# Coarser squares and sums, and buffer fills moved from DVE to POOL, in a fused cosine attention and channel MLP kernel

## The chip, the cores and the metric

The kernel runs on one core of one Trainium2 chip. The metric is the device time of one execution in microseconds (us). A profile covers one execution; its span (602.4 us for the kernel before) is some 1.8 us shorter than the time of the same run. Engines are called as the profile calls them: PE does matrix products, DVE vector work, ACT activation functions and copies, POOL general work and some of the DMA issues, SP DMA issues only.

## The reference

For each of 8 batches and 12 heads, with 448 tokens of 64 elements, the rows of q and k are divided by their norms, scores over tau = 0.1 go through a softmax, and v is averaged by it. The result, as 448 x 768 per batch, goes through a rank-32 mixing of tokens and an MLP over channels (768 to 3072 and back).

```python
q_n = q / (norm(q) + 1e-06); k_n = k / (norm(k) + 1e-06)
attn = softmax(q_n @ k_n.T / tau)
x = heads_side_by_side(attn @ v)              # (8, 448, 768)
u = x + ((x.T @ U) @ V).T
out = u + relu(u @ w_ch1) @ w_ch2             # float32
```

## The kernel before

The kernel doesn't write its instructions in order. It makes a list of operations, each with an engine (or a choice, "ACT/DVE"), an expected duration, what it depends on and which buffers it takes. A greedy planner in the kernel, a small simulation in Python, then decides the order on each engine. Three parts of it matter here. The first is the statistics of q and k: squares, sums, then 1/norm and the scaling (`norm`). `G` is four heads.

```python
def squares(b, g, ld, ops, lo, ii, ss, pr, on, hold, then):
    red = []
    for i in ii:                                  # q, k
        for a0 in range(0, g, G // 2):            # two heads at a time
            a1 = min(g, a0 + G // 2)
            sq = Slot(r_sq, 1)
            o = Op(on, 0.48 if on == "ACT" else 0.44, None,
                   deps=[ops[i], *hold], acq=[sq], prio=pr + 0.2, fast=True)
            # ... o squares, on ACT or DVE
            red.append(plan.add(Op("DVE", dve_t(256 * (a1 - a0)), ..., # reduce_sum
                deps=[o, *then], acq=[ss], rel=[sq], prio=pr + 0.1)))
```

The second is the rule of the planner for when an operation is ready, and the choice that follows: an engine that is free takes the first ready operation by priority.

```python
LAG = {"PE": 0.16, "ACT": 0.10, "DVE": 0.07, "POOL": 0.0, "SP": 0.0}
safe = 0.25                                       # 0.8 while the attention of batches 1 to 7 is listed

def ready_at(self, op, eng):
    t = 0.0
    for d in op.deps:
        # ... None if d has no place yet
        if d.by == eng:
            t = max(t, d.start if eng == "PE" else d.end)   # d.end includes LAG
        else:
            t = max(t, d.end + self.SEM + (op.safe if eng == "PE" else 0.0))
    # ... the same for buffers that have to come free
```

The third is a ring of three PSUM buffers named "mm". The transposes of the scaled q and k (`flip`, tile `tp`), the MLP's matmuls and the small mixing products all draw on it. The first group of batch 0's second MLP matmul takes all three for 3 x 24 matmuls.

```python
tp.tile = psum.tile([128, len(ins) // wide, n], BF, name="tp", tag="mm", bufs=3)   # flip
...
groups = [work[:3]] if b == 0 else []                                              # mlp
for group in groups:
    mms = [Slot(r_mm, 1) for _ in group]
```

The order in which batch 0 is listed, with the fills that the change moves:

```python
fourth = load_qk(0, 8, 12)                        # heads 8 to 11, the last load of batch 0
v_set = [fill(lambda: set_v(v_t[0]), 1000, prio=-1.4)]
begun = stats_first(*first)                       # heads 0, 1
...
begun_2 = stats(0, 2, 4, *second, hold=begun[:2], then=begun)
xn_set.append(fill(lambda: nc.vector.memset(xn_t[2][:, 0:8, :], 0.0), 900, prio=0.41, deps=begun))
z = fill(lambda: nc.vector.memset(V_sb, 0.0), 500, prio=3, deps=begun)
zf = fill(lambda: nc.vector.memset(U_f(), 0.0), 400, prio=0.5, acq=[uv], deps=begun)
...
stats(0, 4, 8, *third, hold=last_exp["first"], then=begun_2)
late = stats(0, 8, 12, *fourth)
load_w1(0, 6)
load_w1(6, 12)
v_set.append(fill(lambda: set_v(v_t[1]), 1000, prio=3, deps=late))   # batch 1's v
```

## Time and profile before

| | before |
|---|---|
| time, median of 3 runs | 603.91 us (603.87 to 603.91) |
| span of the profiled run, granted clock | 602.4 us, 1.0 |
| PE busy, idle | 584.4 us, 18.0 us |
| of the idle: 0 to 30 us, and 500 us to the end | 11.2 us, 3.5 us |
| DVE, ACT busy | 300.0, 278.8 us |
| first matmul of batch 0's MLP | 38.7 us |

In the views below, a row of the timeline has the start in us, the length in us, engine, line, operation, output<-input, shapes and count; in brackets is the idle time of the engine just before and what ended it. Rows of neighbouring instructions on one engine overlap by some hundredths, so lengths can't be added where starts are shown. A row of the busy table has the stretch and its length, then busy us with instruction counts of PE, weight loads, DVE, ACT and POOL, then the granted clock of PE, the DMA share and GB/s. The prediction shows both for this kernel. One more row is used later, of the view by tile, the first matmuls of batch 0's MLP (count, shortest/mean/longest ns, from when to when):

```profile
L762 PE MATMUL sc<-uT,w_sb x18: 323/326/337, 38.7 to 42.8; 128*128 128x384 bf16 x18
```

From that matmul on PE has MLP work to fill every hole, so the time falls into two terms that I use throughout: the **start**, up to this row (38.7 us), and the **rest**, the span minus the start (602.4 - 38.7 = 563.7 us).

### The profile page before, as it was taken

The numbers are of one execution on the slowest core, as the hardware profiler recorded it, in microseconds if no ns is written. First come the engines' busy times: TensorE is split into PE (matmuls) and PEld (weight loads), VectorE is DVE, ScalarE is ACT, GpSimd is POOL, SyncE is SP. The second block draws the span as 40 slices with busy tenths as digits, with TensorE's granted clock in tenths as the row PEclk, the third lists the DMA queues.
The fourth block names the chain that finished last, engine by engine and source line by source line (L and its number), as shares of the span: only waits on it lengthen the run. The fifth ranks groups of instructions, "written<-read, shape, count | busy, mean of one in ns | idle before, by whom it ended". The sixth has DMA issues, their size and how long they took to land.

```text
span 602.4 us, 11513 instructions
## 1 busy us (share of the span) xinstructions
PE 584.4 (97%) x4702; PEld 346.9 (58%) x4725; DVE 300.0 (50%) x722; ACT 278.8 (46%) x604; POOL 114.2 (19%) x175
## 2 busy tenths in 40 slices
PE   4899999999999999999999999999999999999997
PEld 2566766555565665666545666566545666654465
DVE  8979849999998987654721244024300210110011
ACT  7967752577874377316741067505642025014300
POOL 8246334062703406000600000000000000000000
PEclk9999999999999999999999999999999999999999
DMA  9999999999998969715912132030002110310021
GB/s 138 197 181 117 203 202 125 164 135 136 161 167 114 181 104 150 103 56 95 127 20 66 53 73 47 1 93 27 15 1 53 52 40 1 90 41 1 0 53 54
DMA packets 150165, 54.81 MB, mean 91 GB/s; under 512 B 115040, under 2 KB 150112, under 8 KB 150112
## 3 DMA queue, kind: packets, MB, share of 16 engines
q0 software_dynamic: 72864, 25.73, 39.1%
q1 hardware_dynamic: 77184, 28.32, 25.3%
q8 instruction: 37, 0.61, 0.4%
q14 instruction: 16, 0.13, 0.1%
q10 hardware_dynamic: 64, 0.02, 0.0%
HBM read 52.25 MB, written 11.01 MB: 105 GB/s over the span
## 4 chain that ended last, share of the span: by engine, by line
PE 91%; DVE 4%; DMA 2%; ACT 1%; issue 1%; POOL 1%; ACTq 0%; DVEq 0%; POOLq 0%
PE mm L796 36%; PE mm L762 34%; PE sc L572 10%; PE av L594 8%; PE mm L686 1%; DVE xn L536 1%; DMA v_nat<-in_v_dram 1%; DMA qk_nat<-in_q_dram 1%; DVE ss L461 1%; PE tp L374 1%; PE mm L651 1%; ACT attn L577 1%; PE sc L762 0%; POOL qk_nat L396 0%; ACT relu L785 0%
## 5 line engine op out<-in xcount | busy, mean ns | idle before, releaser
L762 PE MATMUL mm<-uT,w_sb 128*128 128x384 bf16 (+1 forms) x1112 | 236.7, 353 | 1.2 <-ACT relu L785 0.2
L796 PE MATMUL mm<-w_sb,relu 128*128 128x384 bf16 (+1 forms) x1368 | 231.9, 324 | 0.3 <-DVE O_sb L805 0.3
L577 ACT ACTIVATE attn<-sc 128x448 bf16<-128x448 f32 x336 | 164.3, 547 | 107.5 <-PE av L594 53.9
L796 PEld LDWEIGHTS <-relu 128*128 128x128 bf16 x1368 | 132.6, 98 | 86.5 <-issue 0.2
L762 PEld LDWEIGHTS <-w_sb 128*128 128x128 bf16 x1152 | 112.1, 98 | 103.9 <-issue 1.4
L785 ACT ACTIVATE relu<-mm 128x512 bf16<-128x512 f32 (+1 forms) x158 | 86.6, 548 | 129.1 <-PE mm L762 128.5
L805 DVE TENSOR_TENSOR O_sb<-mm,u_nat 128x384 f32<-128x384 f32 (+1 forms) x57 | 31.1, 549 | 211.6 <-PE mm L796 208.2
L572 PE MATMUL sc<-qkT 128*128 128x448 bf16 x336 | 104.4, 361 | 3.1 <-ACT attn L577 1.5
L594 PEld LDWEIGHTS <-attn 128*128 128x128 bf16 x1536 | 62.1, 98 | 17.5 <-issue 2.7
L418 POOL DMA_DIRECT2D v_nat<-in_v_dram x98 | 63.2, 654 | 33.2 <-DMA w_sb<-in_moe_w_ch_dram 15.7
L594 PE MATMUL av<-v_nat,attn 128*128 128x65 bf16 x1536 | 66.1, 195 | 0.4 <-DVE X_sb L603 0.2
L461 DVE TENSOR_REDUCE ss<-sq 112x8 f32<-112x512 bf16 x96 | 63.0, 673 | 0.6 <-ACT sq L455 0.4
L536 DVE TENSOR_TENSOR xn<-qk_nat,inv 112x512 bf16<-112x512 bf16 x94 | 60.8, 681 | 0.6 <-DMA qkT<-xn 0.4
L396 POOL DMA_DIRECT2D qk_nat<-in_q_dram x24 | 17.2, 716 | 134.3 <-DVE xn L536 72.9
L603 DVE TENSOR_TENSOR X_sb<-av,rd 128x256 bf16<-128x256 f32 x96 | 40.0, 420 | 1.6
L572 PEld LDWEIGHTS <-qkT 128*128 128x128 bf16 x336 | 28.5, 98 | 20.6 <-issue 5.7
L601 DVE RECIPROCAL rd<-av 128x4 f32<-128x4 f32 x96 | 17.1, 179 | 38.4 <-PE av L594 37.6
L457 DVE TENSOR_TENSOR sq<-qk_nat 112x512 bf16<-112x512 bf16 x89 | 34.2, 413 | 0.5 <-DMA qk_nat<-in_q_dram 0.5
L700 DVE TENSOR_TENSOR u_nat<-mm,X_sb 128x384 bf16<-128x384 f32 x36 | 19.1, 552 | 14.4 <-PE mm L686 14.2
L787 DVE TENSOR_SCALAR relu<-mm 128x384 bf16<-128x384 f32 (+1 forms) x31 | 18.7, 605 | 12.4 <-PE mm L762 11.9
L374 PE MATMUL tp<-ident,xn 112*128 112x112 bf16 x144 | 11.7, 227 | 8.6 <-DVE xn L536 8.2
L474 ACT ACTIVATE ln<-ss 112x32 f32<-112x32 f32 (+2 forms) x26 | 5.9, 228 | 30.3 <-DVE ss L461 30.3
(61 smaller groups left out, 167.8 us busy)
## 6 DMA issues: line engine op xcount, KB each, us to landing
qk_nat<-in_q_dram POOLq DMA_DIRECT2D x23, 224.0 KB, 5.6
qk_nat<-in_k_dram POOLq DMA_DIRECT2D x23, 224.0 KB, 7.0
w_sb<-in_moe_w_ch_dram POOLq DMA_DIRECT2D x4, 1152.0 KB, 14.4
w_sb<-in_moe_w_ch_dram POOLq DMA_DIRECT2D x8, 576.0 KB, 16.2
out_dram<-O_sb SPq DMA_DIRECT2D x15, 168.0 KB, 2.3
out_dram<-O_sb SPq DMA_DIRECT2D x16, 144.0 KB, 2.1
out_dram<-O_sb SPq DMA_DIRECT2D x16, 120.0 KB, 2.0
out_dram<-O_sb SPq DMA_DIRECT2D x16, 96.0 KB, 2.2
```

The costliest lines, as they stand in the source:

```text
L418: nc.gpsimd.dma_start(out=vb[p0:p0 + s1 - s0, hs, j, 0:D], in_=v[b, hs].rearrange("h (s c) d -> c s h d", c=SC)[c, s0:s1]),
L457: nc.vector.tensor_mul(y, x, x)
L461: lambda i=i, a0=a0, a1=a1, sq=sq: nc.vector.reduce_sum(ss.tile[:, i, a0:a1, :].rearrange("p h c -> p (h c)"), sq.tile[:, 0:a1 - a0, :].re ...
L536: nc.vector.tensor_mul(dst, src, sc)
L572: nc.tensor.matmul(out=sc.tile[:, 0:S], lhsT=kT[:, 128 * m:128 * (m + 1)], rhs=qkT.tile[:, 8:12, :].rearrange("p c s -> p (c s)"), start=T ...
L577: exps[m] = plan.add(Op("ACT", act_t(S), lambda sc=sc, m=m: nc.scalar.activation(out=attn.tile[:, m, off:off + S], in_=sc.tile[:, 0:S], fu ...
L594: nc.tensor.matmul(out=av.tile[:, t, 0:D + 1], lhsT=attn.tile[:, m, 128 * t:128 * (t + 1)], rhs=v_t[b % 2][:, h, j, 0:D + 1], start=(j == ...
L603: muls.append(plan.add(Op("DVE", dve_t(256), lambda av=av, rd=rd, h=h: nc.vector.tensor_mul(X.tile[:, :, h * D:(h + 1) * D], av.tile[:, :, ...
L762: o = plan.add(Op("PE", pe_t(n), lambda cc=cc: nc.tensor.matmul(out=mm.tile[:, 0:n], lhsT=w1_sb[:, cc, f * 128:(f + 1) * 128], rhs=uT.tile ...
L785: nc.scalar.activation(out=relu.tile[:, f, 0:n], in_=mm.tile[:, 0:n], func=AF.Relu)
L796: nc.tensor.matmul(out=mm.tile[:, 0:c1 - c0], lhsT=relu.tile[:, f, i * 128:(i + 1) * 128], rhs=w2_t[:, f, c0:c1], start=(f == 0), stop=(f ...
L805: nc.vector.tensor_add(out=O.tile[:, 0:w], in0=mm.tile[:, 0:w], in1=us[i].tile[:, c0:c1]),
```

## The change

Four heads of q or of k are squared in one operation and summed in one, instead of in two each; the expected durations for the planner follow. The zero fills of U, V and the third unit buffer go from DVE to POOL's queue, behind the last q,k load of batch 0. The fill of batch 1's v buffer waits for the last attention multiply of batch 0. The intent is to take work from DVE, which is above 90% busy while PE starves, before 30 us.

```diff
-    r_sq = ring(2, [SCH, G // 2, SC * D], BF, "sq")
+    r_sq = ring(2, [SCH, G, SC * D], BF, "sq")
@@ squares
-            for a0 in range(0, g, G // 2):
-                a1 = min(g, a0 + G // 2)
+            for a0 in range(0, g, G):
+                a1 = min(g, a0 + G)
                 sq = Slot(r_sq, 1)
-                o = Op(on, 0.48 if on == "ACT" else 0.44, None,
+                n = 256 * (a1 - a0)
+                o = Op(on, {"ACT": act_t(n), "DVE": dve_t(n, 1.45)} if "/" in on else act_t(n) if on == "ACT" else dve_t(n, 1.45), None,
@@ batch 0
     fourth = load_qk(0, 8, 12)
+    zf = plan.add(Op("POOL", 0.4, lambda: nc.gpsimd.memset(U_f(), 0.0), acq=[uv]), pool_q)
+    xn_set.append(plan.add(Op("POOL", 0.6, lambda: nc.gpsimd.memset(xn_t[2][:, 0:8, :], 0.0)), pool_q))
+    z = plan.add(Op("POOL", 0.4, lambda: nc.gpsimd.memset(V_sb, 0.0)), pool_q)
...
-    xn_set.append(fill(lambda: nc.vector.memset(xn_t[2][:, 0:8, :], 0.0), 900, prio=0.41, deps=begun))
-    z = fill(lambda: nc.vector.memset(V_sb, 0.0), 500, prio=3, deps=begun)
-    zf = fill(lambda: nc.vector.memset(U_f(), 0.0), 400, prio=0.5, acq=[uv], deps=begun)
...
-    v_set.append(fill(lambda: set_v(v_t[1]), 1000, prio=3, deps=late))
...
     after = last_mul[-1:]
+    v_set.append(fill(lambda: set_v(v_t[1]), 1000, prio=3, deps=after))
```

## The prediction

> **What bounds the kernel now.** I read the page's busy shares first, then busy time by stretches, then the chain of waits of the first 64 us, then the timeline of the first 60 us, because only there does anything but TensorE (PE) matter.
>
> ```profile
> PE 584.4 (97%) x4702; PEld 346.9 (58%) x4725; DVE 300.0 (50%) x722; ACT 278.8 (46%) x604; POOL 114.2 (19%) x175
> PE 91%; DVE 4%; DMA 2%; ACT 1%; issue 1%; POOL 1%; ACTq 0%; DVEq 0%; POOLq 0%
> ```
>
> PE is busy 584.4 of 602.4 us, so all engines together can give back at most 18 us without less matmul work. The busy table by stretches (columns: busy us and instructions of PE, weight loads, DVE, ACT, POOL, then clock, DMA share, GB/s) tells where those 18 us are:
>
> ```profile
> 0.00:10.00 10.00, 2.53 (x15) 1.42 (x16) 7.82 (x24) 5.63 (x15) 8.58 (x17) 1.00 0.97 130
> 10.00:20.00 10.00, 7.84 (x60) 4.37 (x59) 9.09 (x23) 9.42 (x24) 4.03 (x6) 1.00 1.67 171
> 20.00:30.00 10.00, 8.41 (x111) 5.28 (x108) 9.77 (x32) 9.35 (x25) 2.99 (x5) 1.00 1.17 203
> 30.00:40.00 10.00, 9.94 (x164) 6.94 (x165) 6.98 (x22) 8.00 (x19) 5.33 (x8) 1.00 1.13 166
> ```
>
> The first 30 us hold 7.5 + 2.2 + 1.6 = 11.3 us of PE idle, the last stretch (500 to 603) 4.15, and everything from 40 to 500 about 3.3. From 10 to 30 us DVE and ACT are both above 90% busy: together they set when batch 0's attention ends and when batch 0's MLP matmuls (L762) start, in a closed row from 40.69 us. After that PE has MLP work to fill in and hardly stops. So a microsecond of DVE work counts before about 30 us and next to nothing later. The chain of waits there (start, us, what):
>
> ```profile
> 4.66 6.66 DMA v_nat<-in_v_dram
> 11.32 0.28 issue
> 11.60 4.89 DMA qk_nat<-in_q_dram
> ...
> 16.59 0.76 DVE sq L457 x2
> ...
> 19.16 2.40 DVE xn L536 x4
> 21.56 0.30 DVE qkT L828
> 21.86 1.19 DVE ss L461 x2
> ...
> 28.98 0.07 DVE v_nat L838
> ...
> 29.14 0.22 DVE v_nat L842
> ...
> 30.02 0.27 PE av L594 x3
> ```
>
> Up to 16.5 us the end is set by loads: the loads of v hold the queue and q,k of heads 8 to 11 land at 16.49. From 16.59 to 30.02 every step is DVE: squares, sums, scaling, copies. From 30.02 PE is full. The fill of batch 1's v buffer (L838 to L842, 28.97 to 29.68) sits inside that DVE stretch, with an attention multiply (L603) waiting behind it.
>
> **What the Trainium skill says.** (1) "Perfetto Trace Analysis", Optimizing Scalar/DVE Operations: each instruction has a fixed cost, about 60 ns on DVE and 93 ns on ScalarE from SBUF, and the row of an instruction also shows a tail that the next one overlaps. The trace agrees: one sum is 677 ns, but two in a row take 1.27 us, so 0.594 us from start to start; one square is 417 ns and two take 0.755, so 0.34. With one element per DVE cycle of 0.96 GHz (the page "VectorE: DVE Perf Modes", Specifications) 512 elements are 533 ns and the fixed part of a sum is 60 ns; the square at two per cycle is 267 ns plus 73. (2) The same page of trace analysis, Identifying the Most-Contended Engine, warns that matmul busy time is a poor measure of headroom; here the 4.15 us of the last stretch and the 97% therefore only bound the gain from above. (3) "SBUF — State Buffer", Who interferes with whom: GpSimd and DVE share a port pair only for two-port DVE modes, or two SBUF inputs against a GpSimd read; sums never contend. A fill only writes, so I expect little friction between the moved fills and the squares and sums. No sizeable POOL fill is in the trace to check it.
>
> **The change part by part.**
> Squares and sums: a call with four heads issued two squares and two sums for q and two of each for k; now one of each. There are 2 such calls in batch 0 and 3 in each of 7 later batches, 23 in all; the first two calls of batch 0 have two heads and stay as they are. Each call saves 2 x 60 ns of sums and 2 x 73 ns of squares, 0.27 us. Sums go from 96 to 50, at about 1.13 us start to start and a row of 1.21; squares on DVE from 89 to about 44 to 46, 0.61 start to start and a row of 0.68. All in all 23 x 0.27 = 6.1 us off DVE, but 21/23 of that lies after 38 us, beside a full PE. On the path: the two calls of batch 0, 0.5 us, of which some goes back because the steps are coarser (a square of 1,024 must end before its sum can start: 0.61 instead of 0.34).
>
> Fills: the third unit buffer (0.48 us at 8.40), U (0.27 at 10.02) and V (0.30 at 10.30) leave DVE, 1.05 us before the wait for the last q,k load. They delay now the first sums of heads 2,3; but DVE idles 0.51 us before 16.59 and the load is not moved, so I count a third to a half of it, 0.4 us. Batch 1's fill of v, 0.71 us from 28.97 to 29.68, goes behind the last multiply of batch 0 (38.25): this one is directly on the path, though ACT, which works nearly without a gap from 22 to 31 us, can take part of it. I count 0.4.
>
> ```profile
> 8.40 0.48 DVE L900 MEMSET xn<- 112x512 uint32 x1
> 10.02 0.27 DVE L902 MEMSET raw_uv<- 128x256 f32 x1
> 10.30 0.30 DVE L901 MEMSET V_sb<- 128x288 uint32 x1
> 10.32 3.28 SPq L857 DMA_DIRECT2D raw_uv<-in_moe_U_dram  x7
> 27.70 0.29 POOL L863 CAST U_sb<-raw_uv 128x128 bf16<-128x128 f32 x1 [4.16 <-DMA raw_uv<-in_moe_U_dram]
> ```
>
> POOL pays: its fill of the identity, 128 bf16 a partition, took 0.231 us and a one-element fill 0.10, so some 1.03 ns an element. U (256) is then 0.36 us; the unit buffer and V 0.63 and 0.40 as 512 and 288 words, or 1.16 and 0.69 if POOL fills 1,024 and 576 halves: 1.4 to 2.2 us in sum. They stand behind the last q,k load (issued until 13.02), so no load of batch 0 moves; the first weight load goes from 13.01 to about 14.4 to 15.2. The loads of U now wait for POOL's fill of U: from 10.32 to about 13.4, and with SP issuing without a break the last cast of U from 27.70 to some 29.5 to 30.8. Batch 1's q,k and the second half of the first weights, behind that cast in POOL's queue, move by 2 to 3 us (28.28 to about 30.5). Their first use is the square at 39.10, and the weights of f = 12 are needed at about 51, so I take this delay as hidden.
>
> Sum: 0.2 (coarser but fewer squares and sums) + 0.4 + 0.4 = 1.0 us before PE fills up, and 0.1 to 0.2 from the small PE gaps up to 160 us, where DVE is about 95% busy. 603.9 - 1.1 = 602.8.
>
> **Rivals.**
> (a) ACT is the bound from 10 to 30 us and takes the whole gain. For it: 9.42 and 9.35 us of 10 busy, and the exponentials run from 26.99 to 31.5 without a stop. Against it: squares and copies can go to either engine, so what leaves DVE relieves ACT too. Then 603.5 to 604.
> (b) The later loads bite: POOL's queue is 2 to 3 us later, and v of batch 1, whose loads wait on the queue at 41.68 and 49.82, is needed by the first attention product at 62.46. For it: ACT idles 0.96 us at 63.13 for just that. Against it: PE has MLP matmuls beside it and no gap there. If it did bite, 0.5 to 3 us: 604 to 606.
> (c) Coarse DVE operations (1.13 us sums where an eviction of PSUM waits) open gaps in PE from 40 to 300 us; or the order that the kernel's own planner finds, which shifts everywhere when durations change, is luckier or unluckier. The gaps up to 500 us are 3.3 us in all, so luck is worth a microsecond either way.
> (d) The gain is larger: all 1.05 us of early fills, 0.71 of the late one and 0.5 of the squares carry through, 2.3 us: 601.6.
>
> **Range and chances.** Nothing here reaches 2% (12 us): the PE idle that the change touches is 11.3 us, 7.2 of which is the start, before any operation that changes. The range 600.9 to 604.8 takes in (a), (d) with luck, and a mild (b). Faster by over 2%: 0.01. Slower by over 2%: 0.01, were a later load to stop PE repeatedly. Within: 0.98.
>
> **What would show it right or wrong.** Right: 50 sums of some 1.2 us and DVE busy near 293 us; no DVE fill between 8 and 30 us; the closed row of L762 starting about 39.7 instead of 40.69; the start of U's loads near 13.4 and batch 1's q,k load near 30.5; PE busy within 2 us of 584. It is wrong if the row of L762 starts no earlier (then ACT or a load bounds that stage), if PE shows new waits on DMA between 40 and 120 us (rival b), or if PE's idle after 40 us grows beyond 4 us plus the last stretch (rival c).

## The result, and the profile after

The changed kernel takes 604.62 us in the median of 4 runs (604.25 to 605.29), against 603.91 (603.87 to 604.85) for 4 runs of the kernel before. The ratio is 1.0009, with a 95% interval of 0.9992 to 1.0027: the same. Here and below a ratio is not quite that of the medians that I quote. The ratio of the plain means lies within 0.0002 of it everywhere but in g_pause. A thousandth is 0.6 us.

So the time lies in the range, and "within 2%" is right, but of the gain of 1.1 us there is nothing. The page shows that the operations changed as intended:

```profile
PE 586.0 (97%) x4702; PEld 347.7 (58%) x4725; DVE 295.9 (49%) x630; ACT 277.9 (46%) x601; POOL 116.3 (19%) x178
...
L462 DVE TENSOR_REDUCE ss<-sq 112x16 f32<-112x1024 bf16 (+1 forms) x50 | 58.0, 1166 | 0.8 <-ACT sq L456 0.4
```

There are 50 sums, 92 DVE instructions fewer than before and 4.1 us less of DVE work. PE is busy 1.6 us longer than before with the same 4702 recorded matmuls, which is the first odd thing. The busy table has the second:

```profile
10.00:20.00 10.00, 7.77 (x56) 4.38 (x54) 9.59 (x17) 8.36 (x21) 5.18 (x8) 1.00 1.45 158
20.00:30.00 10.00, 9.12 (x114) 6.41 (x115) 9.68 (x27) 7.98 (x21) 2.10 (x3) 0.83 1.12 202
30.00:40.00 10.00, 9.84 (x154) 6.44 (x150) 5.93 (x18) 9.10 (x21) 7.06 (x10) 1.00 0.97 140
```

DVE is as busy between 10 and 30 us as before, and the granted clock from 20 to 30 us is 0.83 instead of 1.00. PE's 9.12 busy us there are not more work but the same work at a lower clock. And the MLP starts later, by the view by tile:

```profile
L763 PE MATMUL sc<-uT,w_sb x18: 324/326/338, 39.6 to 43.7; 128*128 128x384 bf16 x18
```

The start is 0.9 us later (39.6 against 38.7) and the rest is 0.5 us shorter (602.8 - 39.6 = 563.2 against 563.7); together that is the 0.4 us between the spans. To see why the start is later, here is the timeline after the last q,k load has landed, first the kernel before, then after:

```profile
19.08 2.48 DVE L536 TENSOR_TENSOR xn<-qk_nat,inv 112x512 bf16<-112x512 bf16 x4
...
19.81 0.97 PE L374 MATMUL tp<-ident,xn 112*128 112x112 bf16 x12 [0.74 <-DVE xn L536]
...
21.79 1.27 DVE L461 TENSOR_REDUCE ss<-sq 112x8 f32<-112x512 bf16 x2
```

```profile
17.64 0.68 DVE L458 TENSOR_TENSOR sq<-qk_nat 112x1024 bf16<-112x1024 bf16 x1
...
18.51 1.16 DVE L462 TENSOR_REDUCE ss<-sq 112x16 f32<-112x1024 bf16 x1
19.58 2.48 DVE L537 TENSOR_TENSOR xn<-qk_nat,inv 112x512 bf16<-112x512 bf16 x4
...
20.32 0.97 PE L374 MATMUL tp<-ident,xn 112*128 112x112 bf16 x12 [1.65 <-DVE xn L537]
```

PE waits in both for the scaling (xn) of heads 4 to 7. Before, DVE scales as soon as it can, and the sums of k for heads 8 to 11 come after it, at 21.79. After, the planner has put the square of all four heads of k and its sum of 1.16 us ahead of the scaling. From the square of q of heads 8 to 11 to the scaling takes 19.08 - 16.59 = 2.49 us before, and 19.58 - 15.71 = 3.87 us after (the square begins at 15.71 there, because in this run the load had landed earlier). PE's hole grows from 0.74 to 1.65 us. Of these 0.9 us, 0.5 is the later transposes (20.32 against 19.81); the other 0.4 comes from the other end, as PE had run out of the work of heads 0 to 3 at 18.67 instead of 19.07.

The clock comes next. In the trace's record it drops to 0.50 for 3.413 us, once, right after that hole. The busy table in stretches of about that length, before and then after:

```profile
18.70:22.10 3.40, 2.35 (x36) 1.63 (x34) 3.40 (x8) 2.52 (x6) 0.00 (x0) 1.00 1.15 213
22.10:25.50 3.40, 2.60 (x37) 1.55 (x36) 3.33 (x11) 3.40 (x12) 0.97 (x1) 1.00 1.28 216
```

```profile
18.70:22.10 3.40, 1.51 (x20) 1.03 (x20) 3.40 (x6) 1.49 (x5) 0.51 (x1) 1.00 1.20 231
22.10:25.50 3.40, 3.38 (x32) 2.50 (x33) 3.40 (x9) 2.79 (x7) 1.30 (x2) 0.50 1.27 223
```

PE was busy 2.35 of 3.4 us before, and 1.51 of 3.4 after; the next stretch then runs at half the clock, and a score matmul that takes 0.35 us (at 23.15 before) takes 0.56 (at 24.49 after). The Trainium skill, in "TensorE: Matmul & The Clock Gate", Part 1: The HAM clock gate, tells of just this: a free-running window of 4096 cycles, 3413 ns, after which the clock is set to 4/8 or 8/8 by how busy PE was in it. The trace agrees to the nanosecond and to the factor. Only, the page lets the clock fall after an idle window, and here a window with PE 44% busy was enough.

The rest of what was moved went as planned. POOL's fills:

```profile
12.39 0.34 POOL L896 MEMSET raw_uv<- 128x256 f32 x1
12.64 0.98 POOL L897 MEMSET xn<- 112x1024 bf16 x1
13.53 0.60 POOL L898 MEMSET V_sb<- 128x576 bf16 x1
```

They take 1.92 us in sum; the loads of U start at 12.76 and batch 1's q,k load is issued at 30.12. PE has no wait on DMA between 40 and 120 us.

**The theory after this look.** The planned order makes the start later: DVE does a coarse sum first, on which nothing urgent depends, and PE's longer hole then also costs a stretch of half clock. **Rivals:** (1) the clock alone does it, and the order is harmless because DVE is busy throughout anyway; (2) it is chance in the planner's order later on, and the start has nothing to do with it; (3) the fills on POOL do harm.

### The profile page after: what moved, and what is told of

Read it like the earlier page. It is cut to its first block, busy times and chain, and to the rows that moved or that the text cites. A ratio compares the mean times of both kernels' runs of the same rounds, so it can differ in the third digit from the quotient of the medians. Undisturbed runs are those within 1.5% of the kernel's fastest.

```text
span 602.8 us, 11404 instructions
## 1 busy us (share of the span) xinstructions
PE 586.0 (97%) x4702; PEld 347.7 (58%) x4725; DVE 295.9 (49%) x630; ACT 277.9 (46%) x601; POOL 116.3 (19%) x178
## 4 chain that ended last, share of the span: by engine, by line
PE 89%; DVE 7%; ACT 2%; issue 1%; DMA 1%
PE mm L763 35%; PE mm L797 32%; PE sc L573 10%; PE av L595 7%; DVE ss L462 2%; DVE xn L537 2%; PE tp L374 1%; PE mm L687 1%; ACT attn L578 1%; DVE sq L458 1%; DVE u_nat L701 1%; PE mm L652 1%; DVE O_sb L806 1%; PE sc L763 1%; DMA raw_uv<-in_q_dram 1%
## 5 line engine op out<-in xcount | busy, mean ns | idle before, releaser
L573 PE MATMUL sc<-qkT 128*128 128x448 bf16 x336 | 106.6, 364 | 1.8 <-ACT qkT L827 0.6
L462 DVE TENSOR_REDUCE ss<-sq 112x16 f32<-112x1024 bf16 (+1 forms) x50 | 58.0, 1166 | 0.8 <-ACT sq L456 0.4
L602 DVE RECIPROCAL rd<-av 128x4 f32<-128x4 f32 x96 | 17.1, 179 | 38.6 <-PE av L595 37.9
L458 DVE TENSOR_TENSOR sq<-qk_nat 112x1024 bf16<-112x1024 bf16 x45 | 29.8, 671 | 0.0
L788 DVE TENSOR_SCALAR relu<-mm 128x384 bf16<-128x384 f32 (+1 forms) x32 | 19.7, 615 | 14.6 <-PE mm L763 13.8
L701 DVE TENSOR_TENSOR u_nat<-mm,X_sb 128x384 bf16<-128x384 f32 x36 | 19.1, 552 | 15.5 <-PE mm L687 15.4
```

The lines of the kernel that those rows point to most:

```text
L458: nc.vector.tensor_mul(y, x, x)
L462: lambda i=i, a0=a0, a1=a1, sq=sq: nc.vector.reduce_sum(ss.tile[:, i, a0:a1, :].rearrange("p h c -> p (h c)"), sq.tile[:, 0:a1 - a0, :].re ...
L573: nc.tensor.matmul(out=sc.tile[:, 0:S], lhsT=kT[:, 128 * m:128 * (m + 1)], rhs=qkT.tile[:, 8:12, :].rearrange("p c s -> p (c s)"), start=T ...
```

## The experiments

Twelve kernels ran, in three calls of four; the kernel before ran 9 times in each call on the same chip, with medians of 604.51, 604.08 and 604.46 us. All gave the right result. The column "interval" below is the time from DVE's or ACT's first square of heads 8 to 11 to the scaling of heads 4 to 7, in the profiled run; "start" and "rest" are as above. The last column has the mean granted clock of each timed run: 1.0 or .999 means that no whole stretch of half clock occurred, .997 or .996 about one of 3.4 us, .994 two, .989 four (one such stretch is 0.5 x 3.4 / 603 = 0.003). Of the times that the theories under test foretold, those of g_pause and e_halves0 came true, t_after's is at the edge, those of t_fills and t_before were missed by 0.1 to 0.2 us, and those of c_warm, d_order, a_squares, b_fills, i_samelag and t_halves_warm by more.

| kernel | time, us | ratio to before (95%) | interval | start | rest | clocks of its runs |
|---|---|---|---|---|---|---|
| before (profile of the first run) | 603.91 | 1 | 2.49 | 38.7 | 563.7 | 1.0 |
| after | 604.62 | 1.0009 (.9992-1.0027) | 3.87 | 39.6 | 563.2 | .997 .996 .996 .996 |
| c_warm | 604.13 | 0.9999 (.9987-1.0012) | 3.89 | 40.5 | 563.2 | 1.0 1.0 .997 .999 1.0 |
| g_pause | 605.23 | 1.0012 (.9998-1.0025) | 3.69 | 41.9 | 563.7 | .994 .996 1.0 .996 .997 |
| d_order | 607.11 | 1.0039 (1.0026-1.0052) | 2.57 | 39.2 | 566.0 | 1.0 .999 1.0 1.0 .997 |
| a_squares | 607.46 | 1.0054 (1.0042-1.0067) | 4.25 | 40.7 | 564.7 | .997 1.0 .997 .994 1.0 |
| after_again | 604.52 | 1.0011 (.9997-1.0025) | 3.87 | 39.5 | 563.2 | .996 .997 .997 .994 .994 |
| b_fills | 613.65 | 1.0154 (1.0134-1.0174) | 2.49 | 38.7 | 574.2 | .989 .994 .989 .994 |
| e_halves0 | 603.62 | 0.9985 (.9972-.9999) | 3.09 | 39.3 | 563.5 | .997 1.0 .997 .994 .997 |
| i_samelag | 614.92 | 1.0182 (1.0168-1.0196) | 1.28 | 38.6 | 576.2 | .992 .994 .994 .994 |
| t_fills | 604.40 | 1.0002 (.9989-1.0014) | 2.49 | 38.2 | 564.4 | .999 .997 1.0 1.0 .996 |
| t_before | 604.63 | 1.0007 (.9994-1.002) | 2.84 | 38.3 | 564.1 | 1.0 .999 .999 1.0 .997 |
| t_after | 604.80 | 1.0009 (.9996-1.0023) | 3.89 | 40.5 | 563.4 | .994 .996 .997 .997 .996 |
| t_halves_warm | 604.73 | 1.0007 (.9995-1.002) | 3.08 | 38.0 | 564.9 | .999 1.0 1.0 1.0 1.0 |

### c_warm: the changed kernel, with spare work for PE ahead of the scaling

Twenty spare transposes of the identity stand in PE's queue ahead of the transposes that wait for the scaling. They go into the tile that the next transposes overwrite, so nothing else changes, and the planned order is that of after.

```diff
+                if warm_at[0]:                     # counts down to the transposes of heads 4 to 7
+                    warm_at[0] -= 1
+                    if warm_at[0] == 0:
+                        for _ in range(20):
+                            nc.tensor.transpose(out=tp.tile[0:128, 0, :], in_=ident[0:SCH, :],
+                                                identity=ident[:SCH, :SCH])
                 nc.tensor.transpose(out=tp.tile[m * (z % wide):m * (z % wide + 1), z // wide, :], in_=x(),
```

> The changed kernel with its planned order kept, plus 20 spare transposes of the identity put into PE's queue ahead of the transposes of heads 4,5 (they fill the idle 18.66 to 20.32 us and write a PSUM tile that the real ones overwrite). Clock theory (the longer PE idle let the granted clock drop to 0.5 from 22.1 to 25.6 us, which cost the gain): mean clock 1.000 instead of 0.997, scores of 22 to 25 us at 0.35 us instead of 0.56, closed row of L763 about 1.0 to 1.5 us earlier than 41.63, time 603.1 to 603.7. Rival (ACT and DVE set that stage, the clock is a bystander): clock back at 1.000 but time within 0.3 us of the changed kernel, 604.3 to 604.9.

Measured: 604.13 us, ratio 0.9999. Four of five runs have no stretch of half clock, where all nine timed runs of the changed kernel (after and after_again) have one or two. So the drop comes from how little PE does around this hole, and some spare work there prevents it in most runs. The time goes back to that of before, about 0.7 us below after (0.9999 against 1.0009 and 1.0011, with intervals that overlap), but not to the prediction's 0.998. The profiled run shows what is left, in the timeline:

```profile
16.64 0.69 DVE L466 TENSOR_TENSOR sq<-qk_nat 112x1024 bf16<-112x1024 bf16 x1 [1.19 <-DMA qk_nat<-in_q_dram]
...
17.61 1.15 PE L380 MATMUL tp<-ident 112*128 112x112 bf16 x20
...
20.53 2.48 DVE L545 TENSOR_TENSOR xn<-qk_nat,inv 112x512 bf16<-112x512 bf16 x4
...
21.26 0.97 PE L382 MATMUL tp<-ident,xn 112*128 112x112 bf16 x12 [2.51 <-DVE xn L545]
```

Here the load lands at about the time of before, and DVE has been idle 1.19 us for it. The fills that left DVE have turned into waiting for the load. The scaling comes 3.89 us later, as in after, and the MLP starts at 40.5 us at full clock. The clock is part of the loss, then, and not the whole: rival (1) falls.

The spare work did not fill the hole: it ran at once, and PE then idled 2.51 us, longer than in after. The trace's record of the clock tells where its stretches of 3.413 us begin, so PE's work can be counted in them. Here the hole fell into two stretches, both busier than the one of after (1.52 us, from 18.72):

```profile
16.92:20.33 3.41, 1.84 (x41) 1.58 (x38) 3.38 (x6) 0.92 (x3) 0.42 (x1) 1.00 1.09 138
20.33:23.75 3.42, 2.19 (x27) 1.49 (x28) 3.42 (x10) 2.17 (x7) 0.00 (x0) 1.00 1.21 233
```

### g_pause: the kernel before, with DVE held up ahead of the scaling

Two fills of a spare tile stand ahead of the scaling of heads 4 to 7; nothing else of the kernel before changes, the planned order included.

```diff
+                if b == 0 and p == 2 and i == 1:
+                    nc.vector.memset(pause, 0.0)       # 128 x 512 float32, twice
+                    nc.vector.memset(pause, 0.0)
                 nc.vector.tensor_mul(dst, src, sc)
```

> The kernel before with two idle fills of DVE (512 f32 each, about 1.0 us together) put ahead of the scaling of heads 4 to 7 at 19.1 us, so that PE's idle there grows from 0.74 to about 1.7 us as in the changed kernel. Clock theory: the clock drops as well, mean 0.997, and the time grows by more than the 1.0 us of pause: 605.2 to 606.2. Rival (no clock effect): clock 1.000 and at most the pause itself, 604.2 to 604.9.

Measured: the interval is 3.69 us, so the pause is 1.2 us. The time is 605.23 us, ratio 1.0012, some 0.7 us more (1.1 by the plain means, 1.0019), with an interval that just reaches 1. Four of five runs have the half clock, two stretches of it in the profiled one (605.6 us of span and 607.4 us, the slowest). In that run the rest is that of before, 563.7: what is lost is lost in the start, though this slowest run loses more there (3.2 us) than the median does. This copies the result of the changed kernel without any of its edits: delay the scaling by about as much, and the clock falls and the time rises by about as much. It doesn't split the delay from the clock: the one run at 1.0 took 605.09 us, no less than those with one stretch.

### d_order: the changed kernel, with the scaling put first

```diff
-    stats(0, 4, 8, *third, hold=last_exp["first"], then=begun_2)
-    late = stats(0, 8, 12, *fourth)
+    third_xn = stats(0, 4, 8, *third, hold=last_exp["first"], then=begun_2)
+    late = stats(0, 8, 12, *fourth, then=third_xn)       # sums of heads 8 to 11 after that scaling
```

> The changed kernel with the sums of heads 8 to 11 made to wait for the scaling of heads 4 to 7, so that the 1.16 us sum that stood ahead of that scaling (18.51 us) moves behind it. If the coarse sum in front of the scaling opened the PE gap: gap of 1.65 us shrinks to under 1.0, clock 1.000, time 602.4 to 603.6. Rival (the order does not matter, a later wait takes its place since heads 8 to 11 are then late): 604.2 to 605.0.

Measured: the interval is 2.57 us, as before the change, and the clock stays at 1.0 or nearly so. But the time is 607.11 us, ratio 1.0039: worse. The rest is 566.0 us, 2.8 more than in after, more than the start gave back (0.4). So mending the order at 18 us changed the order at 100 us. In the timeline of d_order two rows show where:

```profile
96.97 1.30 PE L797 MATMUL mm<-w_sb,relu 128*128 128x384 bf16 x7 [1.67 <-DVE O_sb L806]
...
98.10 0.76 PE L374 MATMUL tp<-ident,xn 112*128 112x112 bf16 x12
```

The last transposes of batch 1's q and k run at 98.10; in the kernel before they run at 76.16 and in after at 77.89. This was the first sign that a second cause, in the planner, works apart from the start.

### a_squares and b_fills: each half of the change alone

a_squares is the kernel before with the coarse squares and sums only (the first two parts of the diff); b_fills is the kernel before with the moved fills only (the last part).

> The kernel before with only the squares and sums of four heads in one operation; all fills as before. If the coarse squares and sums alone open the gap and drop the clock: mean clock 0.997 and 604.6 to 606.0. Rival (the fills moved to POOL, with the later loads of U behind them, cost the time): clock 1.000 and 603.3 to 603.9.

> The fills of the change alone (POOL fills U, V and the third unit buffer, batch 1's fill of v later), squares and sums in halves as before. If the coarse steps are what spoilt the change: first MLP matmul (L762) at 37.7 to 38.3 us, against 38.7 before and 39.6 in the changed kernel, and 602.8 to 603.8, about 0.8 us under the kernel before. Rival (the fills on POOL and the later loads of U cost the time): first MLP matmul not before 38.7 and 604 to 605.

Measured: the squares alone cost 3.3 us (1.0054), the fills alone 9.3 us (1.0154), and both together 0.5 to 0.7 us. These parts don't add up, so neither number is what its edit costs in work. a_squares loses in both terms: its interval is 4.25 us, the longest, with 2.0 us more start, and the rest is 1.0 more. In b_fills the start is that of before to the tenth, with the interval of 2.49 us, and all the loss is in the rest, 10.5 us. Rival (3) in its plain form falls with it: POOL's fills don't delay the start.

They do widen PE's hole, from its front. In b_fills PE has run out of heads 0 to 3 at 17.50 us and idles 2.00 us, and the clock is halved from 19.37 us, with an interval no longer than before. PE ran out at 17.0 to 18.7 us in seven kernels with the fills on POOL (after, after_again, b_fills, t_fills, e_halves0, i_samelag, t_after), and at 18.8 to 19.8 in the four with the fills on DVE (before, t_before, g_pause, a_squares). The exception is d_order, where PE waited for DVE's multiplies earlier and ran out at 19.7; two more have spare work there. So the early fills did what they should for the first heads; but the load of heads 8 to 11 came no earlier, and PE waited the longer. A stretch of half clock comes with each half of the change: in three of five runs of a_squares and in all of b_fills. The busy table of b_fills has the greater loss:

```profile
100.00:120.00 20.00, 14.48 (x117) 8.55 (x117) 18.73 (x46) 5.82 (x13) 4.13 (x7) 0.87 0.81 104
```

PE is idle 5.5 of these 20 us, against 0.7 in the kernel before. The timeline shows where it begins, in the transposes of batch 1's first heads, in the kernel before and in b_fills:

```profile
46.70 0.56 PE L374 MATMUL tp<-ident,xn 112*128 112x112 bf16 x8
```

```profile
61.33 0.56 PE L374 MATMUL tp<-ident,xn 112*128 112x112 bf16 x8
```

In b_fills DVE began to scale these heads at 47.60 us. The transposes run 13.7 us later, and from 45.73 to 61.33 PE does MLP and mixing products without a pause. The transposes were left out, not delayed by data. The cause is in the planner's code, and the last experiments test it: the three buffers of "mm" are shared, and after one comes free the planner grants it to an MLP matmul 0.35 us later (0.10 + 0.25) but to a transpose only 0.90 us later (0.10 + 0.8). Whenever an MLP matmul is ready, it takes the buffer first. Then the first group of the second MLP matmul takes all three for 72 matmuls; the last transposes of batch 1 in b_fills come at 95.63. Without batch 1's scores, PE has used up its MLP work by 100 us and starves.

### after_again: the changed kernel once more

> The changed kernel as it is, on the same chip as the next three, since the clock drop turned out to come and go from run to run (2 of 9 runs of the kernel before had it on the chip of the first four experiments). If the drop is what the change provokes: mean clock 0.996 to 0.997 in at least 3 of 5 runs, and in runs without it the time equals that of the kernel before within 0.4 us. If it was the luck of one chip: the drop as rare as before, and the ratio to the kernel before still above 1.0005 if the coarse steps themselves cost the time.

Measured: 604.52 us, ratio 1.0011, half clock in all five runs, interval 3.87, start 39.5, rest 563.2. The first result stands, and the interval is the same to 0.01 us: it is set by the planned order, which c_warm and t_after share (3.89), and not by chance.

### e_halves0: the changed kernel, with batch 0 in halves as before

```diff
-            for a0 in range(0, g, G):
-                a1 = min(g, a0 + G)
+            st = G if b else G // 2
+            for a0 in range(0, g, st):
+                a1 = min(g, a0 + st)
```

> The changed kernel with batch 0's squares and sums in halves of two heads, those of batches 1 to 7 in one operation. If the loss is only in batch 0's coarse steps: first MLP matmul as in the run with the fills alone, 37.7 to 38.5, clock drop rare, and 602.8 to 604.0. Rival (coarse sums in later batches hold up evictions that PE waits for): first matmul early but PE waits after 40 us above 2 us and 604.5 or more.

Measured: 603.62 us (602.31 to 604.56), ratio 0.9985 with an interval of 0.9972 to 0.9999. This is the fastest of all kernels here, and the only one whose interval lies below 1. Undoing the coarse steps in batch 0 alone, 2 of the 23 calls concerned, goes with a gain of some 1.6 us against after (0.0026 of 604). The edit also gives a new later order, so the gain isn't shown to be that of batch 0's steps alone. Two of the three signs of the expectation were missed: the first MLP matmul is at 39.3 us, and the clock drop isn't rare. The profiled run was the slowest of the five; in it the interval is 3.09 us, 0.8 less than in after. The other half of the 1.6 us isn't located, as no profile was taken of a run of 602.3. Four of the five runs still have the half clock: PE's hole is there in this order too.

### i_samelag: the changed kernel, with a planner that sees no lag on the same engine

The planner counts a result as usable 0.07 us after the end of a DVE operation, even for DVE itself. When the 1/norm of heads 4 to 7 has just ended, the scaling isn't ready for 0.07 us, DVE is free, and the ready sum of 1.16 us is taken. This is how the coarse sum gets ahead of an operation of higher priority.

```diff
-                t = max(t, d.start if eng == "PE" else d.end)
+                t = max(t, d.start if eng == "PE" else d.end - self.LAG[eng])
```

> The changed kernel with one line of its planner mended: an operation that depends on one of the same engine counts as ready when that ends, not 0.07 us later. The planned order then has the scaling of heads 4 to 7 ahead of the sums of heads 8 to 11, without any added wait. If the planner's 0.07 us let the 1.16 us sum slip in front: first MLP matmul 1.0 to 1.5 us earlier than 39.6, clock drop rare. Time 602.5 to 603.8 if the rest of the plan is as good as before; up to 606 if the new order opens PE waits after 40 us, as in the run that forced the order.

Measured: the order at 18 us is mended, with an interval of 1.28 us, the shortest of all; the start is 38.6. The time is 614.92 us, ratio 1.0182. The rest is 576.2 us: the last transposes of batch 1 run at 97.08 us, and PE is busy only 16.60 and 16.80 of the two stretches of 20 us from 100 to 140. So the cause of the coarse sum's place is confirmed by the order that came out, and the planner's later order took 13 us (seen in the trace, with three stretches of half clock in it, and not tested with that order mended). It also shows that an earlier scaling alone buys less than its length: the scaling came 2.2 us earlier than in after (17.38 against 19.58) and the start only 1.0 us, as the squares and sums that were put off come later on the same engine.

### t_fills, t_before, t_after: the planner's two rules mended

If the loss in the rest of b_fills is what the code suggests, two edits of the planning undo it: transposes get the same margin as MLP matmuls, and batch 0's second MLP matmul, which takes all three buffers, waits for batch 1's transposes.

```diff
             o = plan.add(Op("PE", took, fn, deps=deps + [id_set] if z == 0 else (), acq=[tp] + acq,
                             rel=rel if z == len(ins) - 1 else []), stream)
+            o.safe = min(o.safe, 0.25)
...
+        if b == 1:
+            flips.extend(done)
...
-                        deps=[done[f], w2_ops[f * len(w2_ops) // NC]],
+                        deps=[done[f], w2_ops[f * len(w2_ops) // NC]] + (flips if b == 0 and f == 0 else []),
```

t_fills is b_fills with these edits, t_before the kernel before with them, t_after the changed kernel with them.

> The run with the fills alone (613.65 us) with two rules of its planner mended: transposes of q and k ask no longer margin after a bank of PSUM comes free than the MLP's matmuls do, and batch 0's second MLP stage, which takes all three banks at once, waits for batch 1's last transposes. If transposes that lost the banks to the MLP (ready at 50, issued at 61 us in that run) were what cost 9.5 us: 602.3 to 604.3, PE waits after 90 us under 2 us, batch 1's scores from about 50 us. Rival (POOL's later loads or fills themselves cost it): above 609.

> The kernel before with the same two rules mended, as the base for the next two. Its plan had its transposes within 1 to 3 us of being ready anyway, so little changes: 602.8 to 604.4. Rival (the old plan lost several us here too): under 602.

> The changed kernel with the same two rules mended. If batch 0's coarse steps and the clock drop are the change's own cost and the planner's luck only hid or added to it: 0.2 to 1.2 us above the same rules on the kernel before, clock 0.994 to 0.997 in most runs, first MLP matmul near 39.6. Rival (planner's luck was all of it): at or under the other, by the 1.1 us of the prediction.

Measured: t_fills takes 604.40 us, ratio 1.0002, where b_fills had 1.0154. Its rest is 564.4 instead of 574.2 us, and the busy table has no hole:

```profile
100.00:120.00 20.00, 19.94 (x120) 10.97 (x120) 19.91 (x47) 6.30 (x18) 3.36 (x5) 1.00 0.96 159
```

Batch 1's transposes run from 48.49 to 79.57 us, instead of from 61.33 to 95.63. So the 9.3 us of b_fills were the planner's grants, and no cost of fills on POOL; the two edits weren't tried apart. t_before (1.0007) shows that the edits don't speed up a kernel whose order was lucky already. With them held, the three can be compared: against t_before the fills alone are 0.0005 less, some 0.3 us, and the whole change 0.0002 more, some 0.1 us (0.3 by the plain means). Both are inside the intervals of about 0.8 us either way. With this source of chance removed, then, neither the fills nor the whole change is seen to move the time by a microsecond. t_after shows the same interval of 3.89 us and the half clock in all five runs.

### t_halves_warm: all findings in one

e_halves0 with the two rules of the planner and the spare transposes of c_warm.

> The candidate: the change with batch 0 in halves, the same two rules mended, and the 20 spare transposes that hold the clock. If the start's gain of the prediction is real once batch 0 keeps fine steps and the clock holds: clock 1.000 in at least 4 of 5 runs, first MLP matmul 37.0 to 38.3, 601.3 to 603.0, under both kernels. Rival (the start's gain is given back later): 603.5 or more with the early first matmul.

Measured: the start is the earliest of all, 38.0 us, and the clock is whole in all five runs, yet the time is 604.73 us, ratio 1.0007. The rest is 564.9 us, 1.4 more than in e_halves0; from 200 to 300 us PE idles 1.04 us, 1.0 of it waiting in a mixing product for DVE's addition to the output (O_sb). The gain in the start was given back by another order. Against t_after, which keeps the coarse steps and the half clock, all this gives 0.1 us by the ratios: what the delay and the clock cost in time stays below what these runs resolve. No version was found that beats both kernels by more than e_halves0 does, and its 0.15% is at the edge of its interval.

## Why the prediction was right or wrong

The number was off by 1.8 us (602.8 against 604.62) and inside the range. Its chances for "within 2%" were right, since 97% of the span was PE's work. That the time stayed within 1 us of before was partly luck: half of the same change alone (b_fills) took 613.65 us, and one line of the planner made it 614.92, 1.5% and 1.8% slower, so the 0.01 for "slower by over 2%" was surer than it should have been.

By its own first sign the prediction was wrong: the closed row of that line starts at 41.63 us, no earlier than 40.69. But the bound that it attached to this sign, ACT or a load, is not the whole of it: the order on DVE came first. Its two other signs of being wrong did not come: no wait on DMA between 40 and 120 us, and PE's idle from 40 to 500 us is 2.4 us (3.2 before). Point by point:

- **What bounds the kernel: right in kind.** Only the time before PE fills up is open, and there the wait is for DVE. g_pause points that way: a pause of 1.2 us on DVE at this place costs about 0.7 us by the ratio, whose interval just reaches 1. But the sum takes DVE's work as what counts there, and what counts is the one operation that PE waits for: c_warm and d_order have the same DVE work, and their intervals differ by 1.3 us. One reading was off: the last stretch holds 3.5 us of PE idle and not 4.15, as the span ends at 602.4 and not at 603 (and 11.3 is 11.2). Nothing rests on it.
- **"The two calls of batch 0, 0.5 us, of which some goes back because the steps are coarser": this step failed.** It entered the sum as 0.2 us gained. The prediction counted the coarse square as 0.61 instead of 0.34 us, ahead of its own sum. It did not ask what the coarse sum could be placed ahead of. The interval went from 2.49 to 3.87 us, in every profile of this order within 0.02 us: 1.4 us lost, 1.6 from what was predicted. e_halves0 undoes this part and gains 1.6 us over after by the ratios, though its interval is only 0.8 us shorter; that the delay is what the time lost is in part argued.
- **Early fills, 0.4 us: not seen in the start.** They left DVE as planned. The prediction itself noted that DVE idles 0.51 us for the load there and counted a third to a half; with the fills alone, DVE idled 0.78 us in b_fills, 0.25 in t_fills, and the square began when the load had landed. That work had slack in front of the load: it brought the end of heads 0 to 3 forward, and PE waited the longer after it (see b_fills). The first square of heads 8 to 11 begins anywhere between 15.4 and 17.1 us in these profiles, by when the load lands, and that moves the start by more than the fills do.
- **Late fill of v, 0.4 us: not seen.** From the scaling of heads 4 to 7 to the MLP takes 38.7 - 19.08 = 19.6 us before and 20.0 in after, c_warm and t_fills. Nothing became shorter in that stretch; PE is at least 98% busy from 30 to 40 us in all of them, so it is plausible that a DVE operation of 0.7 us just ahead of it no longer counted; no run took this fill alone.
- **The clock: not considered.** The prediction read 1.00 in all rows and took it as given. The longer hole brought one or two stretches at half clock in each of the changed kernel's runs. In the first call, the kernel before took 604.89 and 604.94 us in two runs with such a stretch and 604.35 in the mean of the other seven, and in the third 604.99 in two against 604.26. That is 0.6 to 0.7 us, in a comparison of few runs, and agrees with what c_warm gave back. Not every kernel shows it (the fastest run of t_fills has a stretch). My estimate from 81 timed runs, each against the mean of its own kernel and call, without b_fills and i_samelag, is 0.6 us a stretch with a standard error of 0.14; it is a correlation.
- **"The planner's luck is worth a microsecond either way" (rival c): the right rival, far too small.** The order after 40 us moved the rest from 563.2 to 576.2 us. For the change as a whole it happened to be good: 0.5 us less than before. The prediction took the 3.3 us of PE idle up to 500 us as the limit of it. But that is what a lucky order leaves, and an unlucky one can add without such a limit.
- **Counts and sizes: right.** 50 sums at 1.21 us; PE busy 586.0 (within 2 us of 584, though the half clock is in it); U's loads at 12.76 (13.4 foretold), batch 1's q,k load at 30.12 (30.5); POOL's fills 1.92 us (1.4 to 2.2). DVE is busy 295.9 us instead of about 293: the scaling rows came to 1.0 us more, and the planner gave DVE one more relu and one more cast (1.0 and 0.6), which were ACT's.
- **Rivals (a), (b), (d).** ACT wasn't the bound: it worked 8.36 and 7.98 us of the two stretches, less than before, and waited 1.33 us for the coarse sum at 19.70. No later load made PE wait between 40 and 120 us. The larger gain did not come.

In the profiled spans the sum is: later scaling +1.4, the stretch to the MLP +0.4 (with the half clock in it), earlier landing of the load in that run -0.9, the rest -0.5, together +0.4 us, as measured. What stays open: the exact split between the delay and the clock; why the rest of after is 0.5 us shorter, beyond another order in which PE idles 0.8 us less from 40 to 500 us; and half of what e_halves0 gained.

## What to carry to other kernels

When operations are made coarser on an engine that another one waits for, ask not only what each costs in sum but what the larger piece will stand ahead of: the saving of 0.27 us a call was lost five times over in the wait at one place. To keep the fine steps where the other engine starves, and the coarse ones elsewhere, is worth a try; here it gave 0.15% once and nothing in t_halves_warm. Look at the granted clock before and after any change that lengthens a hole in PE's work, and don't read a higher busy share of PE as progress. Where a planner or scheduler makes the order, parts of a change don't add up (3.3 and 9.3 us alone, 0.5 together), so hold the order, or find the rule by which it loses, before a number is put down to an edit.

## What the Trainium skill lacked or had wrong

- "TensorE: Matmul & The Clock Gate", Part 1: The HAM clock gate, has the clock fall after an idle window of about 3.4 us. Here it fell to 0.50 for 3.413 us after a stretch in which PE was busy 1.51 of 3.4 us, with no single hole above 1.65 us. A stretch that was 2.35 of 3.4 us busy kept its clock. No one share divides the two: after 1.84 us it was kept (c_warm, above), after 1.91 it fell (a_squares, from 22.99 us).
- "Perfetto Trace Analysis", Optimizing Scalar/DVE Operations, advises grouping where an engine is saturated, and breaking up where it is not saturated but causes bubbles on others. DVE here was both, 9.59 of 10 us busy and the cause of a bubble on PE of 1.65 us; grouping lengthened the wait there (the interval of 2.49 became 3.87 us), and breaking up again came with 1.6 us by the ratios in e_halves0. The page doesn't tell which advice holds when both are so.
- "VectorE: DVE Perf Modes", Zero memsets can be issued as uint32 (trn2), gives one cycle per element, which at its 0.96 GHz is 1.04 ns. The fills on DVE took 0.485 us for 512 words and 0.272 for 256, so 0.83 ns a word.
- No page has the duration of a fill on POOL. The three fills of after took 0.337, 0.604 and 0.977 us for 256 float32, 576 and 1,024 bfloat16 a partition: 0.83 ns an element in either type, and 0.12 us fixed. The prediction's 1.03 ns, from one small fill and a tiny one, was too slow.
